# Attention scores as one stream of full-bank pieces per batch, with one buffer for the probabilities

## The chip, the cores and the metric

The kernel runs on one core of one Trainium2 chip. The metric is device time in microseconds (us). The engines are named as in the profile: PE (matrix engine; PEld is its loading of weights), DVE (vector engine), ACT (scalar engine), POOL, and SP, which issues most DMAs.

## What is computed

Causal attention with 16 extra "beacon" keys and values that every token sees, followed by a two-layer MLP over all tokens:

```python
B, H, S, Nb, D = (8, 8, 576, 16, 64)
k_all = np.concatenate([beacon_k, k], axis=2)
v_all = np.concatenate([beacon_v, v], axis=2)
scores = scale * np.matmul(q, k_all.transpose(0, 1, 3, 2))
scores = np.where(causal, -1000000000.0, scores)   # beacons are never masked
a = softmax(scores)
x = (a @ v_all) as (B*S, H*D) = (4608, 512)
h = x @ w_in          # 512 -> 2048
r = np.maximum(h, 0.0)
out = (r * r) @ w_out  # 2048 -> 512
```

## The kernel before

**Order of work.** The kernel does not write its instructions down in program order. Every piece of work is an `Op` with engine, estimated duration, priority (lower goes first), dependencies, buffers that it takes and gives back, and possibly a gate. `Order.run` (L69) simulates the engines with these estimates and so fixes each engine's instruction order. When an engine is free, it gets the ready operation of lowest priority whose buffers are free and whose gate is open; if only gated ones are ready, it gets the best of those (L135). The engines then run that fixed order, and semaphores hold back whatever is not ready. In the first 22 us the matrix engine is given filler matmuls (L285) where it has nothing else.

**Attention.** There are 8 batches of 8 heads; heads are taken in pairs (4 pairs per batch, `p = 4 * b + pr`), since 64-row operands of two heads fit in the 128 rows of the array: one head uses rows 0 to 63, the other rows 64 to 127. The 592 keys (16 beacons and 576) are 5 chunks `c` of 128, the last of 80; the tokens are 5 tiles `t` (112, 128, 128, 128, 80). Chunk c is needed by tiles t >= c only, so a pair has six stretches of scores, 1664 columns for each head.

Scores go to two PSUM "strips", each of 2 x 512 fp32 columns (one bank for each head). A **piece** is what fills one strip, and ACT takes the exponential of a piece in one instruction (L637) and writes it to a probability buffer `pt`. From batch 1 on the four pieces of a pair (`WHOLE`, L555) are 496, 464, 416 and 288 columns wide. One **visit** of PE to the scores (one `qk` operation, `emit_qk`, L616, matmuls at L622) does two pieces if both strips are free: pieces 0 and 1, then 2 and 3. Batch 0 (`SPLIT`, L563) has two phases of one and three pieces for each pair, and one piece per visit.

When all pieces of a pair are through, DVE masks the diagonal tiles with a `min` against triangles of 0 and a huge number (`emit_mask`, L643): one instruction takes the diagonals of chunks 0 to 3, which lie 512 columns apart (L648), and one that of chunk 4 (L651). Then PE multiplies probabilities by values (`emit_av`, L665, matmuls at L674; a 65th value column of ones gives the sums), 15 matmuls for each head, and DVE divides (`emit_norm`, L692 and L694). The result is transposed into `xT`, by PE for batches 0 to 2 (L742), by DMA on SP after that.

Queries and keys of batches 0 and 1 are transposed by PE (L478) and copied out of PSUM by DVE and ACT; those of later batches by DMA on SP (L398).

There are four `pt` buffers of 2 x 2048 columns; each pair takes one (`take_pt`, L602) and its second block of value matmuls gives it back. All four are partly set to zero by DVE at the start (L297, L298), as tile 4 is read 128 wide though it has 80 columns.

**MLP.** Nine chunks of 512 tokens: 16 groups of four matmuls for the first layer (L805), relu on ACT or DVE (L821, L823), square on DVE (L830), and 4 x 16 matmuls for the second layer (L840). MLP work has the highest priority numbers, so PE does it when attention has nothing ready. Attention is paced against it by a gate (L591): the work of pair p waits until the MLP's PE time has reached `mlp_chunk_us * (LEAD + PACE * (p - HP))`, with 27.7, -0.4 and 0.245. Both visits of a pair have the same gate.

Of the kernel before, what the change touches and what calls it, by code (L numbers as in the profile page):

```python
# [193 lines left out]
def kernel(  # L194
# [11 lines left out]
    nc = tc.nc  # L206
# [20 lines left out]
    NSTG, NPT, RB = 8, 4, 4  # L227
# [34 lines left out]
    pt = [sb(f"pt{i}", [128, 2, 2048], BF16) for i in range(NPT)]  # L262
# [11 lines left out]
    def wait_for(later, first):  # L274
# [4 lines left out]
        pools={"strip": range(2), "ps": range(4), "stg": range(NSTG), "pt": range(NPT)},  # L279
# [16 lines left out]
    for p in pt:  # L296
        nc.vector.memset(p[:, :, 928:1952].rearrange("p h (a w) -> p h a w", w=512)[:, :, :, 0:96], 0.0)  # L297
        nc.vector.memset(p[:, :, 1824:2048], 0.0)  # L298
# [34 lines left out]
    def t_start(t):  # L333
        return max(0, 128 * t - Nb)

    NPE = 2
    SINGLE = ()
# [212 lines left out]
    whole_off = {}  # L550
    for t in range(NT):
        for c in range(t + 1):
            whole_off[c, t] = ((t_start(t) if t < 4 else 1360) if c == 0 else
                               1744 if c == 4 else 512 * c + 128 * (t - c))
    WHOLE = [Phase(  # L555
        pieces=[
            ([(0, 0, 496, 0)], 0, 496),
            ([(1, 112, 576, 0)], 512, 464),
            ([(2, 240, 576, 0), (0, 496, 576, 336)], 1024, 416),
            ([(3, 368, 576, 0), (4, 496, 576, 208)], 1536, 288),  # L560
        ],
        diag=(0, 512, 0, 4), last=1744, tiles=range(NT), off=whole_off)]
# [3 lines left out]
            diag=(0, 240, 0, 2), last=None, tiles=range(0, 2), off={(0, 0): 0, (0, 1): 112, (1, 1): 240}),  # L566
        Phase(
            pieces=[
                ([(2, 240, 576, 0), (4, 496, 576, 336)], 512, 416),
                ([(3, 368, 576, 0), (0, 240, 496, 208)], 1024, 464),  # L570
                ([(1, 240, 576, 0), (0, 496, 576, 336)], 1536, 416),
            ],
            diag=(512, 512, 2, 2), last=848, tiles=range(2, NT),
            off={(2, 2): 512, (2, 3): 640, (2, 4): 768, (4, 4): 848, (3, 3): 1024, (3, 4): 1152,
                 (0, 2): 1232, (0, 3): 1360, (1, 2): 1536, (1, 3): 1664, (1, 4): 1792, (0, 4): 1872}),
# [4 lines left out]
    def phases(p):  # L580
        return SPLIT if p < NSPLIT else WHOLE
# [4 lines left out]

    def add_pair(b, pr):
        p = HP * b + pr
        qk_ops[p] = []

        def gate(o):  # L591
            if p < HP:
                return True
            return o.progress >= mlp_chunk_us * (LEAD + PACE * (p - HP))

        def deps_of(part):
            if b >= NPE:
                return trans[b, "k"] + trans[b, "q"]
            parts = range(part + 1) if p == 0 else [len(parts_of[b]) - 1]
            return [bk_ev[b]] + [trans_part[b, n, pr, x] for n in parts for x in "kq"]  # L600

        take_pt = add(f"pt{p}", "-", 0.0, None, prio=100.0 * p, deps=deps_of(0), take=("pt", "pt"), gate=gate)  # L602
        av_ops[p] = []
        for n, ph in enumerate(phases(p)):
            add_phase(b, pr, p, n, ph, take_pt, deps_of(n), gate)

    def add_phase(b, pr, p, n, ph, take_pt, qk_deps, gate):
        base = 20.0 * RANK.index((p, n)) if b == 0 else 100.0 * p
        exps = []
        size = 1 if b == 0 or p in SINGLE else 2  # L610
        for i in range(0, len(ph.pieces), size):
            group = ph.pieces[i:i + size]
            cols = sum(max(96, t1 - t0) for mms, _, _ in group for _, t0, t1, _ in mms)
            box = {}

            def emit_qk(e, group=group, box=box):  # L616
                for s, (mms, _, _) in enumerate(group):
                    st = strips[box["qk"].slots[s]]
                    for c, t0, t1, at in mms:
                        for hj in range(2):  # L620
                            hp = slice(64 * hj, 64 * hj + 64)
                            nc.tensor.matmul(  # L622
                                st[:, hj, at:at + t1 - t0],
                                kT[b % 2][hp, pr, 128 * c:128 * c + 128],
                                qT[b % 2][hp, pr, t0:t1],
                                start=True, stop=True,
                            )

            qk = add(f"qk{p}.{n}.{i}", "PE", 0.2 + cols / 2400.0, emit_qk, prio=base + i - (0.0 if b else 1000.0),
                     deps=qk_deps + [take_pt], take=("strip", "strip", len(group)), gate=gate)  # L630
            box["qk"] = qk
            qk_ops[p].append(qk)

            for s, (_, off, width) in enumerate(group):
                def emit_exp(e, off=off, width=width, box=box, s=s):
                    st = strips[box["qk"].slots[s]]
                    nc.scalar.activation(pt[take_pt.held[2]][:, :, off:off + width], st[:, :, 0:width],  # L637
                                         AF.Exp, bias=0.0, scale=scale)

                exps.append(add(f"exp{p}.{n}.{i + s}", "ACT", 0.18 + 2 * width / 1200.0, emit_exp,  # L640
                                prio=(base + i + s) * 1.0e-4 - (30.0 if b else 400.0), deps=[qk], give=(qk, s)))

        def emit_mask(e):  # L643
            P = pt[take_pt.held[2]]
            at, step, m0, m = ph.diag
            last = P[0:LAST, :, ph.last:ph.last + LAST] if ph.last is not None else None
            d = P[:, :, at:at + m * step].rearrange("p h (c w) -> p h c w", w=step)[:, :, :, 0:128]
            nc.vector.tensor_tensor(out=d, in0=d, in1=tri[:, m0:m0 + m, :][:, None].to_broadcast([128, 2, m, 128]),  # L648
                                    op=ALU.min)
            if last is not None:  # L650
                nc.vector.tensor_tensor(out=last, in0=last, in1=tri[0:LAST, 1:2, 0:LAST].to_broadcast([LAST, 2, LAST]),  # L651
                                        op=ALU.min)

        first = 500.0 if p < NSPLIT and n == 0 else 0.0
        dve = 0.15 + 0.14 * ph.diag[3] + (0.25 if ph.last else 0.0)
# [6 lines left out]
        for heads in ([(0, 1)] if p < NSPLIT else [(0,), (1,)]):  # L662
            box = {}

            def emit_av(e, heads=heads, box=box):  # L665
                P = pt[take_pt.held[2]]
                a = ps[box["av"].held[2]]
                for hj in heads:
                    at = (hj - heads[0]) * width
                    for t in tl:  # L670
# [11 lines left out]
            av = add(f"av{p}.{n}.{heads[0]}", "PE", (0.031 if b else 0.035) * nh * sum(t + 1 for t in tl), emit_av,  # L682
                     prio=base - 150 + heads[0] - first,
                     deps=[mask] + [cast[b, "v", c] for c in range(tl[-1] + 1)] + av_ops[p], take=("ps", "av"),
                     give=take_pt if ph is phases(p)[-1] and heads[-1] == 1 else None)
            box["av"] = av
            av_ops[p].append(av)

# [191 lines left out]
    for b in range(B):  # L880
# [27 lines left out]
        for pr in range(HP):  # L908
            add_pair(b, pr)
# [59 lines left out]
```

The softmax here doesn't subtract the row's maximum and nothing guards it: scores larger than these inputs give would overflow.

## Time and profile before

| | us |
|---|---|
| median of the runs shown (4; 342.56 to 343.2) | 342.8 |
| the profiled execution itself | 343.2 |
| its span, first to last instruction | 341.5 |
| PE busy | 336.3 (98%) |
| ACT busy | 189.3 (55%) |
| DVE busy | 173.9 (51%) |
| POOL busy | 90.1 (26%) |
| L805 and L840 (MLP matmuls), summed durations | 133.4 and 133.3 |
| L674 (probabilities by values), summed durations | 39.7 |
| L622 (scores), summed durations, 400 matmuls | 35.2 |

Durations of matmuls overlap (a 512-column matmul lasts 379 ns, and the next one begins long before that has passed), so their sums are no share of the span; what a group costs is read from the times at which it and the next one begin or end. The granted clock of PE is 0.999 of full speed over the span. The span begins with some 23 us in which only batch 0's attention is worked on; from about 74 us on, attention of one batch and MLP chunks alternate in small blocks; from 269 us on only MLP is left.

### The profile page before, as it was taken

The numbers are of one execution on the slowest core, as the hardware profiler recorded it, in microseconds if no ns is written. First come the engines' busy times: TensorE is split into PE (matmuls) and PEld (weight loads), VectorE is DVE, ScalarE is ACT, GpSimd is POOL, SyncE is SP. The second block draws the span as 40 slices with busy tenths as digits, with TensorE's granted clock in tenths as the row PEclk, the third lists the DMA queues.
The fourth block names the chain that finished last, engine by engine and source line by source line (L and its number), as shares of the span: only waits on it lengthen the run. The fifth ranks groups of instructions, "written<-read, shape, count | busy, mean of one in ns | idle before, by whom it ended". The sixth has DMA issues, their size and how long they took to land.

```text
span 341.5 us, 7350 instructions
## 1 busy us (share of the span) xinstructions
PE 336.3 (98%) x2969; PEld 180.3 (53%) x2969; DVE 173.9 (51%) x374; ACT 189.3 (55%) x284; POOL 90.1 (26%) x145
## 2 busy tenths in 40 slices
PE   8999999999999999999999999999999999999995
PEld 7677765544554454545458845444444544444442
DVE  5886875246647963487246743665246502301300
ACT  3886854376548756475347744675557226515611
POOL 9864803315405505041422151212000000000000
PEclk9999999999999999999999999999999999999999
DMA  8999979999999999799989995993210131011002
GB/s 147 204 205 219 205 130 203 230 243 214 184 222 254 178 199 192 184 238 191 160 188 229 211 202 101 235 230 61 87 63 0 29 104 61 2 61 62 2 31 91
DMA packets 143664, 51.70 MB, mean 151 GB/s; under 512 B 130670, under 2 KB 138382, under 8 KB 143630
## 3 DMA queue, kind: packets, MB, share of 16 engines
q1 hardware_dynamic: 135231, 42.25, 61.2%
q0 software_dynamic: 7904, 8.69, 14.8%
q8 instruction: 23, 0.38, 0.5%
q10 hardware_dynamic: 495, 0.30, 0.3%
q14 instruction: 11, 0.09, 0.1%
HBM read 37.22 MB, written 9.44 MB: 137 GB/s over the span
## 4 chain that ended last, share of the span: by engine, by line
PE 97%; DVE 2%; ACT 0%; issue 0%; DVEq 0%; ACTq 0%
PE ps L840 37%; PE ps L805 36%; PE ps L674 9%; PE strip L622 9%; PE ps L285 3%; PE ps L478 1%; PE ps L742 1%; DVE g L830 1%; DVE g L823 0%; DVE qT L320 0%; PE ps L475 0%; DVE pt L648 0%; ACT osb L318 0%; PE ps L423 0%; DVE g L291 0%
## 5 line engine op out<-in xcount | busy, mean ns | idle before, releaser
L805 PE MATMUL ps<-xT,w_in 128*128 128x512 bf16 (+3 forms) x704 | 133.4, 341 | 0.2 <-DVE g L823 0.2
L840 PE MATMUL ps<-w_out,g 128*128 128x512 bf16 x576 | 133.3, 379 | 0.0
L637 ACT ACTIVATE pt<-strip 128x832 bf16<-128x832 f32 (+4 forms) x128 | 103.8, 863 | 48.5 <-PE strip L622 47.9
L805 PEld LDWEIGHTS <-w_in 128*128 128x128 bf16 x704 | 65.5, 98 | 55.0 <-issue 3.1
L821 ACT ACTIVATE g<-ps 128x512 bf16<-128x512 f32 (+2 forms) x119 | 66.8, 561 | 41.1 <-PE ps L805 40.5
L840 PEld LDWEIGHTS <-g 128*128 128x128 bf16 x576 | 52.9, 98 | 60.7 <-issue 2.8
L830 DVE TENSOR_TENSOR g<-g 128x1024 bf16<-128x1024 bf16 (+2 forms) x80 | 53.1, 668 | 60.2 <-ACT g L821 58.2
L320 POOL CAST qk_area<-stg 128x512 bf16<-128x512 f32 (+2 forms) x60 | 38.7, 650 | 63.3 <-DMA stg<-in_q_dram 36.7
L320 POOL CAST vb<-stg 128x512 bf16<-128x512 f32 (+1 forms) x40 | 25.4, 642 | 70.7 <-DMA stg<-in_v_dram 30.0
L674 PEld LDWEIGHTS <-pt 128*128 128x128 bf16 (+1 forms) x960 | 36.1, 98 | 14.1 <-issue 3.4
L318 ACT COPY osb<-ps 128x512 f32<-128x512 f32 x24 | 14.0, 585 | 53.2 <-PE ps L840 51.8
L674 PE MATMUL ps<-vb,pt 128*128 128x65 bf16 (+1 forms) x960 | 39.7, 194 | 0.0
L622 PE MATMUL strip<-qT,kT 64*128 64x80 bf16 (+6 forms) x400 | 35.2, 277 | 0.0
L692 DVE RECIPROCAL rcp<-ps 128x5 f32<-128x5 f32 (+2 forms) x64 | 12.3, 192 | 40.4 <-PE ps L674 40.2
L694 DVE TENSOR_TENSOR xn<-ps,rcp 128x320 bf16<-128x320 f32 (+2 forms) x64 | 31.5, 491 | 2.3
L823 DVE TENSOR_SCALAR g<-ps 128x512 bf16<-128x512 f32 (+2 forms) x41 | 24.7, 611 | 13.8 <-PE ps L805 13.0
L648 DVE TENSOR_TENSOR pt<-pt,tri 128x1024 bf16<-128x1024 bf16 (+1 forms) x36 | 24.2, 671 | 11.2 <-ACT pt L637 11.1
L622 PEld LDWEIGHTS <-kT 64*128 64x128 bf16 x400 | 11.9, 94 | 17.9 <-issue 14.6
L320 DVE COPY osb<-ps 128x512 f32<-128x512 f32 x12 | 8.3, 692 | 16.8 <-PE ps L840 16.4
L285 PE MATMUL ps<-g 128*128 128x256 bf16 (+1 forms) x83 | 11.7, 298 | 1.1 <-DVE warm L292 1.1
L651 DVE TENSOR_TENSOR pt<-pt,tri 80x160 bf16<-80x160 bf16 x32 | 11.5, 360 | 0.0
L365 POOL DMA_DIRECT2D stg<-in_v_dram x10 | 8.6, 861 | 6.5 <-DMA w_in<-in_moe_w_in_dram 5.3
(40 smaller groups left out, 75.3 us busy)
## 6 DMA issues: line engine op xcount, KB each, us to landing
out_dram<-osb SPq DMA_DIRECT2D x17, 512.0 KB, 3.5
stg<-in_q_dram SPq DMA_DIRECT2D x24, 256.0 KB, 4.8
stg<-in_k_dram SPq DMA_DIRECT2D x18, 256.0 KB, 5.0
stg<-in_v_dram SPq DMA_DIRECT2D x18, 256.0 KB, 5.0
w_in<-in_moe_w_in_dram POOLq DMA_DIRECT2D x4, 512.0 KB, 8.0
w_out<-in_moe_w_out_dram POOLq DMA_DIRECT2D x4, 512.0 KB, 10.6
stg<-in_v_dram POOLq DMA_DIRECT2D x6, 256.0 KB, 7.4
stg<-in_k_dram SPq DMA_DIRECT2D x6, 224.0 KB, 4.1
```

Source lines behind the costliest of these rows:

```text
L285: nc.tensor.matmul(ps[bank][:, 0:cols], g[1][:, 0, 0:128], g[1][:, 0, 0:cols], start=True, stop=True)
L320: eng[e].tensor_copy(dst, src)
L622: nc.tensor.matmul(st[:, hj, at:at + t1 - t0], kT[b % 2][hp, pr, 128 * c:128 * c + 128], qT[b % 2][hp, pr, t0:t1], start=True, stop=True,)
L637: nc.scalar.activation(pt[take_pt.held[2]][:, :, off:off + width], st[:, :, 0:width], AF.Exp, bias=0.0, scale=scale)
L648: nc.vector.tensor_tensor(out=d, in0=d, in1=tri[:, m0:m0 + m, :][:, None].to_broadcast([128, 2, m, 128]), op=ALU.min)
L674: nc.tensor.matmul(a[:, at + (t - tl[0]) * (D + 1):at + (t - tl[0] + 1) * (D + 1)], P[0:rr, hj, o:o + 128], vb[b % 2][0:rr, c, 2 * pr + hj ...
L694: nc.vector.tensor_tensor(out=xn[b % 2].rearrange("p t (h d) -> p h t d", d=D)[:, h0:h0 + nh, tl[0]:tl[0] + nt], in0=a[:, :, :, 0:D], in1= ...
L805: nc.tensor.matmul(h[:, lo - spans[0][0]:hi - spans[0][0]], w_in_sb[:, mc, ft * 128:(ft + 1) * 128], xT[:, mc, lo % RING:lo % RING + hi - lo],
L821: nc.scalar.activation(dst, h, AF.Relu, bias=0.0, scale=1.0)
L823: nc.vector.tensor_scalar(out=dst, in0=h, scalar1=0.0, scalar2=None, op0=ALU.max)
L830: nc.vector.tensor_tensor(out=d, in0=d, in1=d, op=ALU.mult)
L840: nc.tensor.matmul(o, G[:, fc, ts * 128:(ts + 1) * 128], w_out_sb[:, fc, :], start=(fc == 0), stop=(fc == NFT - 1))
```

## The change

From batch 1 on, the scores of the four pairs of a batch are laid one after the other in one stream of 4 x 1664 = 6656 columns, which is cut into 13 pieces of exactly 512. A piece can end in the middle of a stretch (its matmul is cut in two) and can hold the end of one pair and the beginning of the next. `STREAM` gives for each pair the order of its stretches (key chunk, first token, last token); chunk 0 is cut by hand into two or three. Pieces are opened two to a visit, so a batch has six visits of two pieces and one of one. The gate and the priority of a visit follow its position in the stream.

The probabilities of a batch go to one buffer of 2 x 8192 columns in place of four of 2 x 2048, pair pr at column 1664 * pr. A visit depends on the value matmuls of the former batch for every pair that it holds. The memsets of the buffers are left out. The diagonals no longer lie evenly, so masking takes two instructions of two diagonals each and one for chunk 4. Batch 0 keeps its pieces and phases; only their places in the buffer change. The core of the diff:

```diff
-    pt = [sb(f"pt{i}", [128, 2, 2048], BF16) for i in range(NPT)]
+    pt = sb("pt", [128, 2, 8192], BF16)
...
-    for p in pt:
-        nc.vector.memset(p[:, :, 928:1952].rearrange("p h (a w) -> p h a w", w=512)[:, :, :, 0:96], 0.0)
-        nc.vector.memset(p[:, :, 1824:2048], 0.0)
...
-    WHOLE = [Phase(
-        pieces=[
-            ([(0, 0, 496, 0)], 0, 496),
-            ([(1, 112, 576, 0)], 512, 464),
-            ([(2, 240, 576, 0), (0, 496, 576, 336)], 1024, 416),
-            ([(3, 368, 576, 0), (4, 496, 576, 208)], 1536, 288),
-        ],
-        diag=(0, 512, 0, 4), last=1744, tiles=range(NT), off=whole_off)]
+    STREAM = [
+        ((0, 0, 112), (3, 368, 576), (0, 240, 576), (1, 112, 576), (2, 240, 576), (4, 496, 576), (0, 112, 240)),
+        ((0, 0, 112), (1, 112, 576), (0, 368, 576), (2, 240, 576), (3, 368, 576), (4, 496, 576), (0, 112, 368)),
+        ((0, 0, 112), (0, 240, 576), (1, 112, 576), (3, 368, 576), (2, 240, 576), (4, 496, 576), (0, 112, 240)),
+        ((0, 240, 576), (0, 0, 112), (1, 112, 576), (2, 240, 576), (3, 368, 576), (4, 496, 576), (0, 112, 240)),
+    ]
+    NPC = HP * PW // 512
...
+            while t0 < t1:
+                n, o = divmod(PW * pr + at, 512)
+                w = min(t1 - t0, 512 - o)
+                PIECES[n].append((pr, c, t0, t0 + w, o))
+                t0, at = t0 + w, at + w
...
+        WHOLE.append([Phase(
+            pieces=[], diag=[(off[0, 0], off[mate, mate] - off[0, 0], 0, 2), (rest[0], rest[1] - rest[0], 1, 2)],
+            last=off[4, 4], tiles=range(NT), off=off)])
...
+    def gate_at(pos):
+        return lambda o: o.progress >= mlp_chunk_us * (LEAD + PACE * (pos - HP))
...
+    CROSS = ()
+    SHIFT = 0.25
...
+    def new_visit(b, n):
+        pos = HP * b + 512.0 * n / PW
+        parts = []
+
+        def emit(e):
+            for s, (bb, m) in enumerate(parts):
+                emit_scores(bb, PIECES[m], strips[qk.slots[s]])
+
+        qk = add(f"qk{b}.{n}", "PE", 0.2, emit, prio=100.0 * pos - 1000.0, take=("strip", "strip"), gate=gate_at(pos - SHIFT))
+        opened.append((qk, parts))
+
+    def add_batch(b):
...
+        for n in range(NPC):
+            if not opened:
+                new_visit(b, n)
+            qk, parts = opened[0]
+            parts.append((b, n))
+            qk.take = ("strip", "strip", len(parts))
+            qk.dur += sum(t1 - t0 for _, _, t0, t1, _ in PIECES[n]) / 2400.0
+            pairs = sorted({mm[0] for mm in PIECES[n]})
+            e = add_exp(f"exp{b}.{n}", qk, len(parts) - 1, 512 * n, 512,
+                        1.0e-2 * (HP * b + 512.0 * n / PW) - 30.0)
+            for pr in pairs:
+                p = HP * b + pr
+                for o in deps_of(b, pr, 0) + av_ops[p - HP]:
+                    if o not in qk.need:
+                        qk.need.append(o)
+                qk_ops[p].append(qk)
+                exps_of[p].append(e)
+            if len(parts) == 2 or n == NPC - 1 and b not in CROSS:
+                opened.clear()
...
         def emit_mask(e):
...
+            for at, step, m0, m in ph.diag:
+                d = P[:, :, at:at + m * step].rearrange("p h (c w) -> p h c w", w=step)[:, :, :, 0:128]
+                nc.vector.tensor_tensor(out=d, in0=d, in1=tri[:, m0:m0 + m, :][:, None].to_broadcast([128, 2, m, 128]),
+                                        op=ALU.min)
+            if ph.last is not None:
+                d = P[0:LAST, :, ph.last:ph.last + LAST]
+                nc.vector.tensor_tensor(out=d, in0=d, in1=tri[0:LAST, 1:2, 0:LAST].to_broadcast([LAST, 2, LAST]),
+                                        op=ALU.min)
```

In the kernel before, a visit had the priority `100 * p + i` from batch 1 on (`base + i`, L629).

## The prediction, made before the changed kernel had run

> **What bounds the kernel now.** I read the page first, its busy times and its chain of work that ended last. The chain is the matrix engine from end to end:
>
> ```profile
> PE 336.3 (98%) x2969; PEld 180.3 (53%) x2969; DVE 173.9 (51%) x374; ACT 189.3 (55%) x284; POOL 90.1 (26%) x145
> ...
> PE 97%; DVE 2%; ACT 0%; issue 0%; DVEq 0%; ACTq 0%
> ```
>
> A busy PE may still hide waits, since the ends of matmuls are modelled. So I asked for the waits of PE alone:
>
> ```profile
> PE ps L285 <- DVE warm L292: 1.1, 1, 1.1
> PE ps L805 <- DVE g L823: 0.2, 1, 0.2
> ```
>
> After the start there is one wait in the whole span, 0.2 us. So only what shortens PE's own stream can help, and everything ACT, DVE, POOL and the queues save is worth nothing by itself. The third view is the chain in a steady stretch, which tells what a visit of the scores (L622) costs PE. Columns: start, length, what.
>
> ```profile
> 148.26 3.56 PE ps L805 x16
> 151.82 0.51 PE strip L622 x4
> 152.34 0.56 PE ps L674 x15
> 152.89 0.86 PE ps L805 x4
> 153.76 0.46 PE ps L674 x15
> 154.22 0.86 PE ps L805 x4
> 155.08 0.41 PE strip L622 x8
> 155.49 4.42 PE ps L805 x20
> ```
>
> Four L805 matmuls of 512 columns take 0.86 us, so a column is 0.86/2048 = 0.42 ns. The first visit has two matmul pairs (the two heads of a pair run side by side on 64 rows each) of 496 and 464 columns: 960 x 0.42 = 0.403 of its 0.51 us; 0.107 is not columns. The second has four pairs of 336, 80, 208 and 80: 704 x 0.42 = 0.296 of 0.41; 0.114 over. And the block **after** a visit is longer too: 15 probability-by-value matmuls take 0.56 after a visit and 0.46 elsewhere; 20 L805 take 4.42 where 20 x 0.215 = 4.30 is due. So each visit costs its columns, plus about 0.11 us on the way in, plus 0.10 to 0.12 on the way out. That is the change of the array from 128 rows to 64 and back, paid per visit, whatever its width.
>
> **The change, part by part.** Profiled execution: 343.2 us, of which 341.5 span and 1.7 around it; the median shown is 342.8. I take differences from this execution and set them against the median.
>
> *Fewer visits.* From batch 1 on, four pairs made 8 visits (pieces 0-1 and 2-3 of each); 13 pieces make six visits of two and one of one, 7. Seven batches: 7 visits less, at 0.11 + 0.10 = 0.21 us: **-1.47 us**. The columns stay: 4 x 1664 = 6656 = 13 x 512. Batch 0 keeps its 16 visits and its shapes.
>
> *More matmuls.* Cutting the stream at multiples of 512 gives, counted from the table, 38 matmul pairs per batch in place of 24, none under 80 columns. The second visit above has two pairs more than the first and 0.007 us more that is not columns: 3.5 ns per added pair; with the rounding of both rows, 0 to 8.5. Another row agrees: 15 matmuls of 65 columns, each with its own weights, take 0.46 us, 31 ns each, against 27 by columns. 14 pairs x 7 batches x 3.5 ns = **+0.34 us** (0 to +0.83). Their weight loads lie beside matmuls: an 80-column pair, the narrowest, is already in the 0.41 row.
>
> The Trainium skill, "TensorE: Matmul & The Clock Gate", section "Back-to-back issue gap", speaks against this part: a stream of weight load and matmul is said to sustain about 81 ns per matmul at 128 columns, where 56 would be the bare gap. Charged with those 25 ns, the 196 added matmuls would cost an estimated 4.9 us and the change would end slower. The row of 31 ns at 65 columns with a load each contradicts that figure here, and I go by the row.
>
> *ACT.* Four exponentials per pair become 13 per batch of 1024 elements. By form they take 996 ns (992 elements), 942 (928), 863 (832) and 651 (576): 3.45 per pair, 13.8 per batch. The slope is 0.83 ns per element, so 1024 take 1.02 and 13 take 13.3: 0.5 us less per batch. Worth 0 on the path: no PE wait names ACT. Without that cover it would be -3.6 in all.
>
> *DVE.* The diagonal's masking goes from one operation of 1024 elements to two of 512:
>
> ```profile
> L648 DVE TENSOR_TENSOR pt<-pt,tri 128x1024 bf16<-128x1024 bf16 x28 | 20.5, 733 | 10.6 <-ACT pt L637 10.5
> ...
> L648 DVE TENSOR_TENSOR pt<-pt,tri 128x512 bf16<-128x512 bf16 x8 | 3.6, 454 | 0.6 <-ACT pt L637 0.6
> ```
>
> 2 x 454 - 733 = +0.18 us per pair, +4.9 in 28 pairs. At 51% DVE and with MLP matmuls for PE to do meanwhile I cost it 0, except in one stretch (below). The eight memsets of the old buffers (1.61 to 3.41 us) go. DVE's first cast then may start 0.1 sooner, but PE's first transpose (4.51) follows ACT's cast (3.96 to 4.36), which waited for its DMA: 0.
>
> *Moved.* The gate of a visit now follows its place in the stream, a quarter pair earlier: 0.25 x 0.245 x 27.7 = 1.7 us of MLP progress. Same PE work in another order: 0. No DMA is added, taken away or moved on a queue. The transposes that feed batch 2 (SP) are issued at 61.1 and 65.7 us and take 5.8 in the median to land, so 71.5; the first visit, 74.6 now, may come at 72.9. Were it late, the MLP block of 40 matmuls before it could go on, so 0. Visits now need the projections of two pairs where a piece spans them. In batch 1 these are PE transposes and copies, done by 38 us.
>
> *One buffer.* An exponential may overwrite only what the former batch's value matmuls have read. Four pairs lie between, as with four buffers. That waits go by the part of a tile and not by the whole is seen on w_in:
>
> ```profile
> L805 PEld LDWEIGHTS <-w_in x704: 95/98/100, 23.5 to 323.2; 128*128 128x128 bf16 x176
> ...
> L767 POOL DMA_DIRECT2D w_in<-in_moe_w_in_dram x4: 751/763/767, 13.6 to 17.9; - x4
> ...
> DMA to landing us min/median/max: 5.9/8.0/10.7
> ```
>
> The last quarter was issued at 17.9 and landed no sooner than 23.8, yet the first reader started at 23.5, though its addresses lie between those of all quarters. I take 0.
>
> **Sum:** -1.47 + 0.34 = -1.13, so 343.2 - 1.1 = 342.1 in a profiled execution, and **341.7** against the median.
>
> **Rivals.**
>
> *Small gain* (chance 0.21). Switches at 0.095 each way where the rows' rounding allows it (7 x 0.19 = 1.33) and pairs at 8.5 ns (0.83): -0.5, 342.3. For it: the rows have two digits. Against it: the blocks after visits show 0.10 to 0.12 again and again.
>
> *Batch 1 becomes bound by ACT and DVE* (0.18; the slower side). From 33 to 48 us PE has little but the first MLP chunk, each of whose results needs ACT or DVE, and both are nearly full (PE, weight loads, DVE, ACT busy):
>
> ```profile
> 33.00:38.00 5.00, 5.00 (x87) 3.23 (x82) 4.04 (x8) 3.52 (x6) 3.87 (x6) 1.00 1.09 209
> 38.00:43.00 5.00, 4.86 (x48) 3.61 (x45) 5.00 (x13) 4.52 (x8) 4.03 (x8) 1.00 1.23 205
> 43.00:48.00 5.00, 4.97 (x62) 3.17 (x62) 4.53 (x14) 3.07 (x6) 0.00 (x0) 1.00 1.15 192
> ```
>
> DVE is idle for 0.00 of the 5 us from 38 to 43, and the one wait of PE sits there. The change puts visits ahead of other PE work (priority lower by 1000), so one visit more may fall into it: two exponentials, 2.05 us, and masks dearer by 0.18 x 3 = 0.5. With nothing free PE idles for up to 2.6: 342.8 - 1.1 + 2.6 = 344.3; at two thirds of that, 343.4. It decides from 1.1 us of new PE waits (no gain) and gives a slower kernel from 1.8. Against it: the work is moved, not added, and the planner counts every operation, so it can give PE something else.
>
> *False waits on the single buffer* (0.04). If waits went by the whole tile, an exponential would wait for the value matmuls just ahead of it: in the rows above a visit ends at 152.34 and the second value block at 154.22, 1.9 us later, of which some 0.8 is slack before the next visit (155.08): 1.0 x 28 pairs, some 370 us. The w_in rows speak against it.
>
> *It does not do what it says*: if visits were split again, L622 would still come in 72 groups, and 0.3 us would be lost. I put it with the small gain.
>
> **Chances and range.** The forecast has 0.57. About 0.2% (0.7 us) is what a measurement of this kernel can tell from no change, so a gain of 1.1 is not far beyond it. Faster by over 0.2%: 0.57; within: 0.21; slower: 0.18 + 0.04 = 0.22. Range: lowest if pairs cost nothing and PE's wait of 0.2 goes (-1.7), less 0.5 for the spread of the runs shown (342.56 to 343.2): 340.6; highest the full second rival, 344.3. It leaves out the false waits and little else.
>
> **What would show it.** L622 in 65 groups (16 + 49) in place of 72, x532 matmuls more in batches 1 to 7 than 336; blocks after a visit still 0.10 longer; PE busy lower by about 1.1; exponentials of 1024 elements x91 at 1.02 us; L648 of 512 elements at 0.45 x64. The waits of PE must stay as short a list as now. Wrong if the list grows in the stretch 33 to 48 (second rival), if ACT waits for PE L674 before exponentials (third), or if a visit's time over its columns rises with its number of pairs by more than 8.5 ns each.

## The result and the profile after

The changed kernel takes **342.5 us** (median of 53 runs, 341.34 to 345.26) against 343.29 of the kernel before (79 runs; the four shown with the prediction had 342.8). The ratio is 0.998, with an interval of 0.9971 to 0.9988: faster by 0.7 us by the ratio (0.8 by the medians) where 1.1 was forecast. The median of 342.8 that the forecast started from was itself 0.5 us low.

The medians hide the more telling part. The table puts together the runs of the unaltered kernels from all comparisons (the two repeats of the kernel before, told below, are left out and would move no figure by more than 0.02; the last row is an experiment, told below too):

| us | runs | 10th percentile | median | 90th percentile |
|---|---|---|---|---|
| before | 216 | 342.82 | 343.36 | 344.08 |
| changed | 78 | 341.67 | 342.44 | 343.82 |
| changed, batch 1's priorities apart | 33 | 341.50 | 342.23 | 342.94 |

At the 10th percentile the changed kernel gains 1.15 us (95% interval 0.98 to 1.25), just the forecast; at the 90th 0.3 (from 0.73 faster to 0.06 slower). So something seems to be lost in some executions and not in others. The one profiled with the result is the slowest of its 53 (345.26 us, span 343.2), and shows much of it.

In the changed kernel scores are L611 (before L622), exponentials L620 (L637), masks L689 (L648), value matmuls L715 (L674), MLP layers L845 and L880 (L805, L840), relu and square on DVE L863 and L870 (L823, L830), batch 1's transposes on PE L475 (L478).

The busy times and the chain that ended last, changed kernel (the durations called summed in the table ahead of the prediction are busy times as well, in which an overlap counts once):

```profile
PE 336.0 (98%) x3165; PEld 185.7 (54%) x3165; DVE 170.6 (50%) x388; ACT 190.3 (55%) x269; POOL 92.0 (27%) x145
...
PE 89%; DMA 5%; POOL 3%; DVE 1%; issue 0%; ACT 0%; POOLq 0%; DVEq 0%; ACTq 0%
```

PE is as full as before, but the chain no longer consists of PE alone: 8% of the span go to DMA and POOL, which is the load of batch 1's keys and, ahead of it in POOL's queue, a load of values and its casts. The waits of PE name it (the 1.1 us are in the start of both kernels):

```profile
PE ps L475 <- DMA qk_area<-in_k_dram: 2.0, 1, 2.0
PE ps L286 <- DVE warm L293: 1.1, 1, 1.1
```

The chain of the changed kernel from 14 to 47 us (start, length, what):

```profile
19.70 11.71 DMA qk_area<-in_k_dram
31.41 0.04 issue
31.46 0.77 PE ps L475 x24
32.23 1.93 PE ps L845 x8
```

and the same place in the kernel before:

```profile
27.56 2.62 PE ps L805 x24
30.19 0.63 PE ps L478 x24
30.82 1.03 PE ps L805 x8
```

with the loads of batch 1's keys and queries in the kernel before:

```profile
L443 POOL DMA_DIRECT2D qk_area<-in_k_dram x2: 699/700/701, 18.6 to 20.0; - x2
...
DMA to landing us min/median/max: 11.0/12.4/13.8
```

In both, batch 1's keys are loaded by POOL's queue and PE transposes them at about 30 us. Before, the first load of keys was issued at 18.63 us and took 11.0 to land, at 29.63, 0.4 us ahead of PE, which was free at 30.0; here it landed at 31.41, and PE, there at 29.3, stood for 2.0 us. The wait has a second price: the same eight MLP matmuls take 1.93 us behind it and 1.03 before. The stretch by the microsecond (PE, weight loads, DVE, ACT and POOL busy, granted clock, DMA share, GB/s) shows why:

```profile
31.00:32.00 1.00, 0.54 (x24) 0.54 (x24) 0.05 (x1) 0.00 (x0) 0.19 (x2) 0.97 1.30 228
32.00:33.00 1.00, 1.00 (x12) 0.63 (x7) 1.00 (x2) 0.00 (x0) 0.84 (x1) 0.50 1.18 279
...
36.00:37.00 1.00, 1.00 (x16) 0.60 (x14) 0.90 (x3) 0.64 (x1) 0.49 (x1) 1.00 1.02 205
```

The granted clock falls to 0.50 and is back at 1.00 by 36 us. This fall is rare: among the 78 runs of the changed kernel the profiled one is the only one with a mean granted clock under 0.997 (0.994), and of the 137 runs of the kernel before that have it on record one has 0.993 (345.64 us). It makes up part of the slowest run and nothing of the median.

What the change itself does can be read in the steady part:

```profile
147.70 0.55 PE strip L611 x14
148.25 0.57 PE ps L715 x15
148.82 4.32 PE ps L845 x20
...
155.10 0.46 PE ps L715 x15
...
159.02 0.33 PE strip L611 x8
159.35 2.69 PE ps L845 x12
```

A visit of seven pairs and 1024 columns takes 0.55 us, of which 1024 x 0.42 ns = 0.43 are columns; the visit of one piece 0.33, of which 0.215. That is 0.12 on the way in, and the block behind is still 0.10 to 0.11 longer (0.57 against 0.46; 2.69 against 12 x 0.216 = 2.59). L611 has 596 matmuls, 64 in batch 0 and 532 after. By form:

```profile
L620 ACT ACTIVATE pt<-strip 128x1024 bf16<-128x1024 f32 x91 | 88.8, 1024 | 38.4 <-PE strip L611 38.4
...
L689 DVE TENSOR_TENSOR pt<-pt,tri 128x512 bf16<-128x512 bf16 x64 | 29.8, 474 | 10.1 <-ACT pt L620 8.9
```

91 exponentials at 1.02 us and 64 masks at 0.47, where 1.02 and 0.45 were forecast.

### The profile page after: what moved, and what is told of

Same layout as the page of the kernel before. It is cut to its first block, busy times and chain, and to the rows that moved or that the text cites. A ratio compares the mean times of both kernels' runs of the same rounds, so it can differ in the third digit from the quotient of the medians.

```text
span 343.2 us, 7716 instructions
## 1 busy us (share of the span) xinstructions
PE 336.0 (98%) x3165; PEld 185.7 (54%) x3165; DVE 170.6 (50%) x388; ACT 190.3 (55%) x269; POOL 92.0 (27%) x145
## 4 chain that ended last, share of the span: by engine, by line
PE 89%; DMA 5%; POOL 3%; DVE 1%; issue 0%; ACT 0%; POOLq 0%; DVEq 0%; ACTq 0%
PE ps L880 37%; PE ps L845 35%; PE ps L715 8%; PE strip L611 7%; DMA qk_area<-in_k_dram 3%; DMA stg<-in_v_dram 2%; POOL qk_area L440 1%; PE ps L475 1%; POOL stg L362 1%; PE ps L782 1%; DVE g L870 1%; POOL w_in L807 0%; POOL vb L318 0%; POOL tri L302 0%; ACT osb L316 0%
## 5 line engine op out<-in xcount | busy, mean ns | idle before, releaser
L845 PE MATMUL ps<-xT,w_in 128*128 128x512 bf16 (+3 forms) x704 | 135.2, 343 | 0.1
L880 PE MATMUL ps<-w_out,g 128*128 128x512 bf16 x576 | 134.4, 379 | 0.0
L620 ACT ACTIVATE pt<-strip 128x1024 bf16<-128x1024 f32 (+3 forms) x107 | 101.9, 1000 | 42.5 <-PE strip L611 42.1
L845 PEld LDWEIGHTS <-w_in 128*128 128x128 bf16 x704 | 66.0, 98 | 52.9 <-issue 1.4
L870 DVE TENSOR_TENSOR g<-g 128x1024 bf16<-128x1024 bf16 (+2 forms) x80 | 53.3, 671 | 69.2 <-ACT g L861 68.3
L880 PEld LDWEIGHTS <-g 128*128 128x128 bf16 x576 | 52.6, 98 | 57.3 <-issue 1.7
L318 POOL CAST qk_area<-stg 128x512 bf16<-128x512 f32 (+2 forms) x60 | 40.9, 688 | 68.3 <-DMA stg<-in_q_dram 35.4
L316 ACT COPY osb<-ps 128x512 f32<-128x512 f32 x27 | 15.8, 586 | 51.1 <-PE ps L880 50.2
L715 PEld LDWEIGHTS <-pt 128*128 128x128 bf16 (+1 forms) x960 | 35.7, 98 | 11.0 <-issue 1.9
L715 PE MATMUL ps<-vb,pt 128*128 128x65 bf16 (+1 forms) x960 | 39.8, 194 | 0.0
L689 DVE TENSOR_TENSOR pt<-pt,tri 128x512 bf16<-128x512 bf16 x64 | 29.8, 474 | 10.1 <-ACT pt L620 8.9
L611 PE MATMUL strip<-qT,kT 64*128 64x208 bf16 (+15 forms) x596 | 34.2, 239 | 0.0
L611 PEld LDWEIGHTS <-kT 64*128 64x128 bf16 x596 | 19.0, 94 | 21.3 <-issue 19.5
L863 DVE TENSOR_SCALAR g<-ps 128x512 bf16<-128x512 f32 (+2 forms) x40 | 23.5, 603 | 9.7 <-PE ps L845 8.8
L318 DVE COPY osb<-ps 128x512 f32<-128x512 f32 x9 | 6.2, 691 | 18.8 <-PE ps L880 18.6
L693 DVE TENSOR_TENSOR pt<-pt,tri 80x160 bf16<-80x160 bf16 x32 | 9.4, 294 | 0.0
```

The lines of the kernel that those rows point to most:

```text
L316: nc.scalar.copy(dst, src)
L318: eng[e].tensor_copy(dst, src)
L611: nc.tensor.matmul(st[:, hj, at:at + t1 - t0], kT[b % 2][hp, pr, 128 * c:128 * c + 128], qT[b % 2][hp, pr, t0:t1], start=True, stop=True,)
L620: nc.scalar.activation(pt[:, :, at:at + width], strips[qk.slots[s]][:, :, 0:width], AF.Exp, bias=0.0, scale=scale)
L715: nc.tensor.matmul(a[:, at + (t - tl[0]) * (D + 1):at + (t - tl[0] + 1) * (D + 1)], P[0:rr, hj, o:o + 128], vb[b % 2][0:rr, c, 2 * pr + hj ...
L845: nc.tensor.matmul(h[:, lo - spans[0][0]:hi - spans[0][0]], w_in_sb[:, mc, ft * 128:(ft + 1) * 128], xT[:, mc, lo % RING:lo % RING + hi - lo],
```

## The experiments

Every ratio below is to the kernel before, run on the same chip. Two theories at the outset: **early limiters** (the work saved on PE is real, but in the first 66 us PE then waits for a load or for DVE), and **mis-sized terms** (a visit is worth less than 0.21 us, or an added pair costs more than 3.5 ns).

**The changed kernel again**, no edit.

> The changed kernel once more, unaltered. In its profiled execution PE waited 2.0 us at 29.5 us for the load of batch 1's keys, and ran for some microseconds at a lower clock after that; the execution took 345.3 us. Theory A (the change itself is worth the forecast 1.1 us, and what is missing of it is lost in executions in which that load comes late): a profile without the wait spans about 341.5 - 1.1 = 340.4 us or less and is faster than before by about 1.1 us; the times lie in two groups, one near 341.7 and one some 1 to 3 us above. Theory B (the terms of the sum were too big): every profile is about 0.7 us faster, with no such groups.

342.32 us, ratio 0.9973 (0.9954 to 0.9992). The key load landed at 30.25 us and PE waited less; a wait for DVE came up:

```profile
PE ps L475 <- DMA qk_area<-in_k_dram: 0.9, 1, 0.9
PE ps L845 <- DVE g L863: 0.4, 1, 0.4
```

So the 2.0 us of the first profile were one draw of several, not a constant of the change, and the half clock did not follow the shorter wait. PE busy is 334.3 us here, 2.0 less than before, where 1.1 was forecast. The two groups of times that theory A (early limiters) expected are not there: the twelve runs spread from 341.76 to 343.68.

**Memsets kept**: the change takes eight memsets from DVE's start; the only difference of the two programs up to 33 us.

```diff
+    for i in range(4):
+        p = pt[:, :, 2048 * i:2048 * i + 2048]
+        nc.vector.memset(p[:, :, 928:1952].rearrange("p h (a w) -> p h a w", w=512)[:, :, :, 0:96], 0.0)
+        nc.vector.memset(p[:, :, 1824:2048], 0.0)
```

> The changed kernel with the eight start memsets of DVE put back (same sizes, on the one buffer). They are all that differs in the first 33 us of the program between the kernel before and the changed one. Theory A1 (their removal lets the start run ahead and so into the late load, or shifts the loads): with them the spread of the times narrows to that of the kernel before, and the kernel is about 1.1 us faster than before, 341.9 to 342.2. Theory A2 (the late load is chance, in both kernels alike): times and spread like the changed kernel, within 0.3 us. Theory B: like the changed kernel.

342.16 us, 0.9971 (0.9958 to 0.9984). The keys landed at 30.91 and PE waited 1.5 us (and 0.5 for DVE, 0.3 for queries). So the load can come late with the memsets too, and leaving them out is worth nothing that these runs can tell, as predicted.

**Eight visits**: pieces 10, 11 and 12 get a visit each; pieces, exponentials and pairs unchanged.

```diff
-            if len(parts) == 2 or n == NPC - 1 and b not in CROSS:
+            if len(parts) == 2 or n >= NPC - 3:
```

> The changed kernel with 8 visits per batch in place of 7 (pieces 10, 11 and 12 one per visit); matmuls, exponentials and masks as changed. If a visit costs 0.21 us beside its columns, 7 x 0.21 = 1.5 us slower than the changed kernel, that is some 0.4 to 0.8 us slower than before (half of the forecast gain was right: the removed visits are the gain). Rival (the gain came from the fewer exponentials or the start): no slower than the changed kernel, within 0.3 us.

344.18 us, 1.0022 (1.0008 to 1.0036): with one visit more per batch, and the exponentials and the start unaltered, the gain is gone. Against the changed kernel on the same chip this is +1.86 for 7 visits, 0.27 us each. From the steady part of the traces (from the first L845 matmul of the second MLP chunk to the end) it is 276.62 against 275.51 us, 0.185 for each of 6 visits. The split visit in the chain:

```profile
151.80 0.33 PE strip L611 x6
152.12 0.56 PE ps L715 x15
...
154.87 0.32 PE strip L611 x4
155.19 2.70 PE ps L845 x12
```

Both halves, of three pairs and of two, cost 0.32 to 0.33 for 512 columns (0.215), and both blocks behind are 0.10 longer. The forecast's 0.21 lies between the two measures.

**Batch 1's loads reckoned late**: the planner is told that they land 2.5 us later, so that it gives PE other work first.

```diff
-                    after = [add_part_load(b, 0, prs, x, prio + n, after, [], 1.5, 1.5)]
+                    after = [add_part_load(b, 0, prs, x, prio + n, after, [], 1.5, 4.0)]
```

> The changed kernel with the planner told that batch 1's query and key loads are seen by PE 4.0 us after they land and not 1.5 (the estimate alone; the loads are issued as before), so that PE's order has more first-layer MLP matmuls ahead of batch 1's transposes. Theory A: the wait of 2.0 us at the first of these transposes goes; times narrow, median about 341.7 or lower, 1.2 to 1.6 us faster than before. Theory B: no better than the changed kernel; or slower, since batch 1's attention starts later and DVE and ACT crowd there.

343.11 us, 0.9999 (0.9985 to 1.0012). PE no longer waited for the keys (its transposes began at 31.7) but 1.8 us for w_out (L880), which the work brought forward needs. The wait was moved, not removed.

**The kernel before again**, for its scatter.

> The kernel before, unaltered, for a second profile of its start. In three profiles of kernels with the changed scores PE reached batch 1's first transposes at 29.2 to 29.3 us and the load of the keys landed at 30.3 to 31.4; in the one profile of before PE came at 30.0 and the load had landed at 29.6. Theory A2 (the late load is chance and meets both kernels): here too a landing later than PE's arrival, or within 0.5 us of it, and the stretch from the first MLP matmul of chunk 1 to the end 275.7 us as in the first profile. Theory A1 (the changed kernel makes it late): landing again at 29.6 or sooner and no wait. Time: no difference from before, within 0.3 us.

343.29 us, 0.9997 (0.9987 to 1.0007). Keys landed at 30.0, PE was there at 29.97 and waited 0.3 us for queries, 0.2 for DVE.

**The kernel before with one buffer**: the four buffers become quarters of one tile, everything else as before.

```diff
-    pt = [sb(f"pt{i}", [128, 2, 2048], BF16) for i in range(NPT)]
+    pt_all = sb("pt", [128, 2, 2048 * NPT], BF16)
+    pt = [pt_all[:, :, 2048 * i:2048 * i + 2048] for i in range(NPT)]
```

> The kernel before with its four probability buffers as quarters of one tile; all else unchanged. If waits go by the whole tile (third rival of the prediction), exponentials wait for value matmuls and the kernel is slower by many microseconds, up to some 28. If they go by parts, no difference from before, within 0.3 us. Its start is that of before, so it is a third look at when the load of batch 1's keys lands.

343.48 us, 0.9999 (0.9985 to 1.0013), with no new wait: the third rival is out.

**Pairs cut**: on the changed kernel every score matmul of 160 or more columns is cut in two, 20 pairs more per batch at the same columns and visits.

```diff
+        if b >= 1:
+            mms = [(pr, c, u0, u1, at + u0 - t0) for pr, c, t0, t1, at in mms for u0, u1 in
+                   (((t0, (t0 + t1) // 2), ((t0 + t1) // 2, t1)) if t1 - t0 >= 160 else ((t0, t1),))]
```

> The changed kernel with every score matmul of 160 columns or more, in batches 1 to 7, cut into two halves: 20 more matmul pairs per batch, 140 in all, same columns, same visits. The prediction's 3.5 ns per added pair gives +0.5 us over the changed kernel; its upper bound of 8.5 ns gives +1.2; nothing per pair gives 0. From the first chunk 1 matmul to the end (batches 2 to 7, 120 pairs) the profile should be 0.42 us longer than the 275.5 of the changed kernel at 3.5 ns.

342.93 us, 0.9992 (0.9979 to 1.0005): 0.49 above the changed kernel's pooled 342.44, over 140 pairs 3.5 ns each, but the interval of this one comparison is 0.45 us to either side. By the steady part it is 0.67 over 120, 5.6 ns, a wait of 0.1 us for a DMA transpose included. The starts of matmuls around a visit give, beyond its columns, 209 and 212 ns at two and four pairs (before) and 213, 217 and 219 at five, six and seven (changed): about 2 ns per pair. The term of 3.5 ns lies between.

**Keys ahead of weights**: batch 1's first load of keys and of queries is issued ahead of the last quarter of w_in.

```diff
-                    after = [add_part_load(b, 0, prs, x, prio + n, after, [], 1.5, 1.5)]
+                    after = [add_part_load(b, 0, prs, x, prio + n, after, [], 1.5, 3.0)]
...
-    strided[1, 0, 0, "k"].behind[:] = chain[-1:]
+    strided[1, 0, 0, "k"].behind[:] = [w_ops["in", 2]]
+    w_ops["in", 3].behind[:] = [strided[1, 0, 0, "q"]]
+    strided[1, 0, 2, "k"].behind[:] = [w_ops["in", 3]]
```

> The changed kernel with the first loads of batch 1's keys and queries (two pairs) issued before the last quarter of the first-layer weights and not after it, and with the planner's estimate of when PE sees them 1.5 us later. Theory A: the wait for the keys goes in every execution, the times narrow, and the kernel is 1.1 us or more faster than before, median 342.0 or lower, with a stretch from the first transposes of batch 1 to the first chunk 1 matmul of 35 us or less. Rival: another load is then late (the last quarter of w_in, w_out, or the second pair of loads), and nothing is won.

342.38 us, 0.9971 (0.9959 to 0.9982). The keys landed at 27.2 and the wait was gone, but the median stayed. The profile has other waits, 0.3 us for w_out (at 50.4 us), as the rival had it, and 0.7 us of the scores for the DMA transposes of batch 6's keys (at 196.8 us). Curing the first limiter alone is not seen in the median.

**Gate unshifted**:

```diff
-    SHIFT = 0.25
+    SHIFT = 0.0
```

> The changed kernel with the gate of a visit at its place in the stream and not a quarter pair earlier (1.7 us of MLP progress later). In profiles of the changed kernel the first visit of batches 6 and 7 comes 0 to 1.5 us after its transposes have landed (before: 5.6 to 9.7 us), and in some PE waits for them. Theory C (this thin margin is part of what is lost and of the wide spread of the times): margins of batches 6 and 7 grow to some 2 us, no PE wait for transposes, and the median is lower than the changed kernel's by 0.2 to 0.5 us. Rival (the spread comes from the first 66 us alone): margin larger, time as the changed kernel, within 0.2 us.

342.47 us, 0.9974 (0.9963 to 0.9985), and PE's list has no wait for DMA or DVE after the start. But the margins of batches 6 and 7, which the edit was to widen to some 2 us, were 0.4 and 1.0 us. The median is that of the changed kernel; the twelve runs lie closer together (341.99 to 343.08).

**DMA transposes reckoned late**: from 3.0 to 6.0 us in the planner, against the wait of the keys' experiment.

```diff
-        trans[b, x] = [add(f"tr{b}{x}", "SP", 4.1, emit, prio=prio, deps=deps, dma=3.7, late=3.0)]
+        trans[b, x] = [add(f"tr{b}{x}", "SP", 4.1, emit, prio=prio, deps=deps, dma=3.7, late=6.0)]
```

> The changed kernel with the planner told that the DMA transposes are seen by PE 6.0 us after they land and not 3.0, which moves only first visits that come right after a landing, and what the planner makes of it. Theory C: margins of batches 6 and 7 of 3 us or more, spread narrower, median lower by 0.2 to 0.5 us. Rival: no difference, or slower, where the later visits delay the next batch's loads on SP.

343.23 us, 1.0004 (0.9987 to 1.0021): the margin of batches 6 and 7 rose from about 1 to 2.4 and 3.1 us, but the new order brought waits of 0.3 to 0.8 us for xn, xT and DVE, and PE waited 0.8 us for batch 1's keys, which this edit does not touch. Not a cure.

**Batch 1's priorities apart**: its visits keep priority 100 per pair, without the 1000 that puts a visit ahead of everything else.

```diff
-        qk = add(f"qk{b}.{n}", "PE", 0.2, emit, prio=100.0 * pos - 1000.0, take=("strip", "strip"), gate=gate_at(pos - SHIFT))
+        qk = add(f"qk{b}.{n}", "PE", 0.2, emit, prio=100.0 * pos - (1000.0 if b > 1 else 0.0), take=("strip", "strip"), gate=gate_at(pos - SHIFT))
```

> The changed kernel with batch 1's visits at the priority of the kernel before (100 times the place, not 1000 less), so that batch 1's transposes and value matmuls go ahead of them as before. The second rival of the prediction (visits put ahead crowd ACT and DVE in batch 1) expects the PE wait on DVE's relu at 41 to 43 us to shrink from 0.4-0.6 us to the 0.2-0.35 of before and the stretch from batch 1's first transposes to chunk 1 to shorten by about 0.3 us. Rival: the crowding comes from the pieces' own size and the third mask, and nothing changes.

342.08 us, 0.9968 (0.995 to 0.9985); no wait for DVE, none for the keys.

**Keys ahead of weights and gate unshifted**, both edits as above.

> Both cures together: batch 1's first loads ahead of the last quarter of w_in (as in the run before with that order) and the gate unshifted. If late loads at the start and the thin margin are what keeps the changed kernel from its forecast, this is the fastest: 1.2 us or more faster than before, median 341.9 or lower, with the highest time under 343.5. Rival (the loss lies elsewhere): like the changed kernel, within 0.3 us.

342.21 us, 0.9969 (0.9953 to 0.9984), highest 343.57, with waits of 1.0 us for batch 0's keys at 15 us, 0.7 for xT and 0.3 for kT. The expected 341.9 was not reached.

Then four kernels on one chip, to set the priorities against the changed kernel directly. The changed kernel:

> The changed kernel as it is, beside the kernel with batch 1's priorities set apart, on the same chip. Theory of two early limiters (the load of batch 1's keys sets its start, and TensorE waits for VectorE's rectified tiles in batch 1): 342.2 to 342.7 us, keys landing after 29.9 us, a wait of 0.3 us or more of TensorE for VectorE's rectified tile between 38 and 45 us. Theory of chance alone: keys land between 28.8 and 31.4 us as in the kernel before (its mean was 29.5 us), and the wait for the rectified tile is there or not as it falls.

342.44 us, 0.9972 (0.9954 to 0.999). The priorities apart:

> Batch 1's score and MLP work keeps the order of priorities that it has without the advance of 1000, as in the run before. Theory of two early limiters: 0.2 to 0.5 us below the changed kernel on the same chip, 341.8 to 342.3 us, and no wait for the rectified tile in batch 1. Rival, that the 0.24 us by which it stood below was the scatter of medians: within 0.1 us of the changed kernel, 342.3 us or more.

342.28 us, 0.9964 (0.9948 to 0.9981). The priorities apart and `SHIFT = 0.0`:

> Batch 1's priorities set apart and the gate of the planner's stream unshifted, both. Theory of two early limiters, if the gate gives something of its own in batch 1: 341.6 to 341.9 us. If both take away the same wait: as with the priorities alone, 341.9 to 342.3 us.

342.0 us, 0.9968 (0.9949 to 0.9986). The kernel before:

> The kernel before again, for its start: if the later landing of batch 1's keys in the changed kernels (30.2 us in the mean over ten profiles, against 29.5 over three) is chance, it lands here anywhere from 28.8 to 31.4 us; if the change brings it, below 30.0 us. Time 343.3 us, within 0.1% of the kernel before.

343.29 us, 0.9996 (0.9984 to 1.0008). The keys landed at 29.64, which either answer allows.

In this run of the changed kernel the keys landed at 29.93, before PE needed them, so that in the stretch from 38 to 43 us the wait for DVE is not mixed with the effects of a late start. Its stretches (PE first, DVE third):

```profile
33.00:38.00 5.00, 4.87 (x87) 3.39 (x80) 3.75 (x8) 3.60 (x5) 3.07 (x5) 1.00 1.08 230
38.00:43.00 5.00, 4.51 (x54) 3.35 (x53) 5.00 (x11) 3.59 (x7) 5.00 (x9) 1.00 1.21 200
```

and with the priorities apart:

```profile
33.00:38.00 5.00, 5.00 (x91) 3.54 (x88) 4.08 (x9) 3.77 (x8) 3.38 (x6) 1.00 1.06 206
38.00:43.00 5.00, 5.00 (x54) 4.16 (x52) 4.90 (x12) 4.37 (x6) 4.36 (x8) 1.00 1.23 205
```

With the advance, PE loses 0.13 us in the first five (at the second load of queries) and 0.49 in the second, while DVE is full from 38 to 43. The chain of the same changed kernel says what DVE did:

```profile
38.29 2.69 DVE g L870 x3
40.98 0.36 DVE g L863
41.34 0.04 issue
41.38 1.03 PE ps L845 x8
```

PE waits for a bank that a relu on DVE (L863) empties, and that relu stands behind three squares. Without the advance DVE is as busy (4.90), but PE has something else in this profile, as in the two others with the priorities apart. That the advance causes the wait does not follow: five kernels that keep it have no wait for DVE there either (loads reckoned late, pairs cut, keys ahead of weights, gate unshifted, and the last two edits together). With the gate unshifted:

```profile
38.00:43.00 5.00, 5.00 (x61) 3.93 (x59) 4.89 (x14) 4.36 (x8) 3.80 (x8) 1.00 1.24 202
```

From batch 1's first transposes to the second MLP chunk, the kernels with cut pairs and with the gate unshifted take 34.4 and 34.1 us, the changed kernel, with waits of 0.4 and 0.5 us, 34.9 and 35.3, and the priorities apart 34.3 and 34.4 (two profiles, less 0.86 us for four L880 matmuls more). So the profiles with the wait are 0.5 to 1.2 us longer there than those without. The cut pairs leave the order of PE's work as it is in the changed kernel, and still the wait does not occur with them.

In the median the priorities were worth 0.16 us on this chip, less than one comparison can tell. Over the three comparisons that set them apart (33 runs, 12 of them with `SHIFT = 0.0` too) and the 78 runs of the changed kernel the medians differ by 0.21, with an interval from 0.72 faster to 0.04 slower, and the 75th percentiles by 0.50 (0.10 to 1.03). Whether `SHIFT = 0.0` adds to it stays open. The two lowest medians of the study are among these, 342.0 us with both edits and 342.08.

The run of 342.28 us shows the third place at which the saved time can be lost:

```profile
223.21 5.86 DMA kT<-qk_area
229.07 0.05 issue
229.12 0.61 PE strip L611 x10
```

The transposes of batch 7's keys are issued at 223.2 us and land at 229.1, after the visit is due: 1.2 us of waiting. In the kernel before (the last line is from its chain, the visit):

```profile
L398 SPq DMA_TRANSPOSE kT<-qk_area x1: 3215/3215/3215, 219.3 to 219.3; - x1
...
DMA to landing us min/median/max: 6.4/6.4/6.5
...
232.19 0.51 PE strip L622 x4
```

There they were issued at 219.3 us, landed at 225.8 and met a visit 6.3 us later (5.3 to 9.7 us in its four profiles for batches 6 and 7). In the changed kernel as it is, the margin was between 0.0 and 1.5 us in each of its three profiles. SP issues the same DMAs as before, but in another order: a store of results (L908) now stands between the transposes of batch 7's queries and keys, where it stood ahead of both. The kernel before has a thin place too, at batch 4: a margin of 0.05 us in two of its four profiles, and in one a wait of 0.3 us. The changed kernel has 3.4 us or more there, so the new order moves the thin place more than it makes one.

## Why the terms were right and the sum was not

**Fewer visits, -1.47, and more matmuls, +0.34: right.** One visit more per batch costs 0.185 to 0.27 us each (forecast 0.21), a pair 2 to 5.6 ns (3.5). In the steady part the kernel before takes 275.68, 275.70 and 275.68 us from the second MLP chunk to the end, the changed one 275.60, 275.51 and (memsets kept) 275.50 with four more L880 matmuls (0.86 us) behind that point: 0.94 to 1.06 less for the same work. Batches 2 to 7 should give 6/7 of 1.13 = 0.97. The fourth profile of each is 0.6 to 0.9 us longer there; both have PE waiting for DMA transposes (0.3 us before, 0.6 changed). So the small-gain rival, which doubted the sizes, is wrong, though the time came out close to where it put it. In the profiles what is missing lies mostly ahead of that point: up to there the four profiles of the kernel before take 65.07 to 66.16 us, the four of the changed one 65.24 to 67.59 with 0.86 us less work, that is 66.1 to 68.45 for the same work, where the forecast had 0.16 less.

The row of 31 ns also decided rightly against the Trainium skill's page "TensorE: Matmul & The Clock Gate", section "Back-to-back issue gap": by its 81 ns per matmul the 280 matmuls added in the experiment with cut pairs would cost an estimated 280 x 25 ns = 7 us (25 ns each as in the prediction); they cost 0.5. Another page, "TensorEngine Tiling (Array Packing)", section "Key Properties", says that changing the tiling mode drains the engine. It gives no price; the eight-visit run prices a visit here at about 0.2 us, there and back. No run shows the drain apart from the rest of a visit.

**"So only what shortens PE's own stream can help": the step that failed.** It took a list of waits from one execution for a property of the kernel. A list with one wait of 0.2 us says that other limiters came second in that execution; it does not say by how much. In the three profiles of the unaltered changed kernel PE waited 2.0, 0.9 and 0 us for the keys, 0.1, 0.4 and 0.5 for DVE in batch 1, and 0, 0 and 0.6 for the transposes of batch 7. The key load was 0.4 us behind PE's own work, and it lands between 28.76 and 30.0 us over four profiles of the kernel before and between 29.93 and 31.41 over three of the changed one. The start of batch 1 is the later of PE's arrival (29.2 to 30.0) and that landing.

**"Same PE work in another order: 0. No DMA is added, taken away or moved on a queue"** is the form that this failure takes in the sum, together with the transposes, which the prediction costed at 0 from batch 2 alone. No DMA is added or taken away, and POOL's queue is as before; but on SP's queue the order of the 162 DMAs is another one. Nor can "the MLP block of 40 matmuls before it could go on" help at a late transpose: PE's order is fixed, and PE stood at such a visit for 0.6 us in the changed kernel and for 1.2 with the priorities apart. The order has its price in two places: the wait for DVE in batch 1 rises from 0.2 us (0.4 in one profile of four) to 0.4 or 0.5 (0.1 where the start was latest), and the margin of the last two batches' DMA transposes shrinks from over 5 us to about 1. The visit of batch 2 that "may come at 72.9" came at 75.7 to 78.1; that cost nothing.

**The second rival was half right.** Its place (38 to 43 us) and engine (DVE) are those that the trace shows, its price of up to 2.6 us was five times too high. Its cause (visits put ahead by 1000) is not shown: without the advance the wait was absent from three profiles of three, with it from five of eleven (and 0.1 us in one more). "The planner can give PE something else" held in those profiles and not in the others. With the advance away, the median of the three kernels' runs lies 1.13 us under the kernel before (0.87 to 1.54): the forecast, to the digit by luck.

**What stays open.** The three waits are shown. That for the keys goes when they are loaded earlier, and that for DVE was absent from every profile with the priorities apart; no edit was a clean cure of that for the DMA transposes. How much of the 0.2 to 0.4 us missing in the median belongs to each is not shown, nor why the wait for DVE comes in some executions. The profiles of the unaltered changed kernel were longer than its median each time (345.26, 342.9 and 343.71 us), so their waits weigh more than the usual ones. Nor is it settled whether the change makes the keys land later. PE waited for them in three of four profiles of the changed kernel (memsets kept among them) and in none of four before, but the programs are alike up to 33 us except for the memsets, the order of POOL's queue is the same, and the changed kernel of the last comparison did not wait. In eight profiles of altered versions, without the memsets and with the order of the loads as it was, they landed between 29.12 and 30.98 us, within the range of the two kernels.

## To carry to other kernels

A short list of waits from one profile shows what came last in that execution; before taking time from the bounding engine, ask of each transfer and each engine how far behind it was, and take another profile. Work that is moved without being added should be costed at every place where its order meets a queue or a nearly full engine, not at the first one. And the percentiles of many runs are worth reading apart: a gain that stands at the 10th and vanishes at the 90th may be one that waits take back in some executions.

## What the runs showed of the hardware

One wait of PE of 2.0 us was followed by a granted clock of 0.50 from about 32 to 35 us: from batch 1's first transposes to its first visit PE took 5.13 us (31.46 to 36.59), against 3.62 for the same work when the changed kernel was profiled again, so 1.5 us were lost beyond the wait. Waits of 1.5 and 0.9 us at the same instruction were not followed by it. The Trainium skill's page "TensorE: Matmul & The Clock Gate", section "What's actually happening", puts the fall after an idle window of some 3.4 us; here 2.0 us were enough once, and the measurement decides. The first load of batch 1's keys, issued between 18.6 and 19.7 us, took from 9.2 to 11.7 us to land in the sixteen profiles that leave the order of the loads alone: a spread of more than twice the gain of the change.
